# A gated mix of a state-space convolution and a squared-ReLU layer with all gradients: fifteen weight-gradient units moved ahead, inverse rows in load order, a denser pace of dense steps, later parameter gradients

## The chip, the cores and the metric

The kernel runs on one core of one Trainium2 chip. The metric is the device time of one execution in microseconds (us); lower is better. The engines are TensorE (PE; its weight loads PEld), VectorE (DVE), ScalarE (ACT), GpSimd (POOL) and SyncE (SP). DMAs are issued by SP, ACT or POOL, each in the order of its own program.

## The reference

The forward pass mixes two branches with a gate per position, and the reference returns its output and the gradients of fourteen inputs. x is 2048 x 448, the state-space part has 256 states per channel, the dense part 1792 hidden units, all in bf16.

```python
g = sigmoid((x * gate_w).sum(-1, keepdims=True))
# branch A: K[d, l] = Re(sum_n C[d, n] * exp(dt[d] * A[d, n] * l) * dt[d] * B[d, n])
#           y = irfft(rfft(x, 4096) * rfft(K, 4096))[:2048] + x * Dskip
# branch B: out = relu(x @ w1 + b1) ** 2 @ w2 + b2
out = g * a + (1 - g) * b
_out, _vjp = jax.vjp(_f, ...)      # then every gradient for grad_out
```

## The kernel before

**Layout.** Positions lie as 16 tiles of 128 (`LT`), channels as 448 columns (`D`); hidden units are 14 blocks of 128 (`FT`). Large SBUF tiles are reused by tag: a new tile of a tag waits until the last reader of the old one is done. The order of work of all engines from the first chunk on is written out by hand; nothing reorders it.

**The convolution.** It is a two-step transform over 64 x 64 positions. `fwd1` (L233) makes the first step in eight steps n = 0 to 7, each copied from PSUM by ACT and DVE (L207, L208, L217, L219) and stored to HBM (`gd`); `between(n)` (L1444) is called after each of them. `fwd2` (L254) loads it back and makes the second step. `cmul` (L266 to L271) multiplies spectra on DVE. `inv1` (L285) makes the first inverse step with the constant matrix `MI` and stores its rows to HBM (`hd`); `load_hs` (L294) loads a quarter of them with two DMAs, one for each half of the partitions, and `inv2` (L303) makes the second step. There are three inverses: `hd[0]` early, for the correlation that the filter's gradient needs (L660), `hd[1]` for the output `out_0`, and `hd[2]` for the gradient of x, `out_1`.

**The chunks.** The 14 chunks of 32 channels are worked in `period(c)`, L1158, c = 1 to 13, and a closing `period(14)`. In a chunk DVE builds two power tables X and Y by doubling (L707 to L721); TensorE turns them (L802, L816), multiplies them to kernel rows (`kgen`, L775), and forms the group products Z of the chunk before (L856), which DVE multiplies with a table (L872) and TensorE sums (L889) to the sums S and T. In the last chunk the kernel rows go to HBM (L790, `k_d`) and come back as the filter in `xs` (L1243); the transform of the filter, `fwd1` at L1448, follows `period(14)`. `s_out` (L906) stores S and T, and the parameter gradients load them later (`load_st`, L1359 and L1360).

**The dense steps.** `dense()` (L948) is a generator of 126 steps: the hidden units (L969), the projection (L996), the gradient of the hidden units (L1100) with its gate on DVE (L1076, `gate_rows`), and the projection back (L996 again). It keeps its results in HBM: hidden rows in `rT_d`, gated gradient rows in `dhT_d`, the branch rows of both projections in `br_d`. `De(x)` (L1127) raises the number of steps that are due by x and runs the steps that are missing. A live chunk asks for 9.7. `ahead()` (L1148), called in the last chunk behind the first half of the last table step, runs all that are left, loads the output gradient into `Gt`, a tile of tag U16 (L1153), and the first three blocks of hidden rows.

**The units.** Two weight gradients, `out_12` (from `rT_d`) and `out_10` (from `dhT_d`), are made in 125 units by the generator `units()`. `turn(i, th)` (L1268) transposes eight 128 x 128 pieces of block i to PSUM, and ACT or DVE copies them back (L1272, L1270); `mul_rows(i, th)` (L1281) makes eight matmuls of 448 columns; `turn_back` (L1298) turns a finished block of `out_10`. `Fl(n)` runs n units. All of them lie behind `period(14)`: ten in `between`, the rest between the steps of the tail, and `Fl(200)` at the end runs what is left. The first 14 blocks multiply with `DB2`, the output gradient scaled by 1 - g, which DVE makes from `Gt` in `between(0)` and `between(1)` (L1447) into a tile of tag Y16.

**The parameter gradients.** `param_grads(dt)` (L1371) is a generator of DVE work for four blocks of channels; its first instruction adds T to S (L1379). `Pg(n)` runs n of its segments: one after each of the eight steps of `fwd1`, and the rest before the products. Blocks 2 and 3 come with the last inverse; their tile `Dw`, of tag Y16, is loaded by SP (L1345) behind the product `GU` (L1573), which reads `Gt`, and ahead of the first `load_hs` of `hd[2]`.

**The tail in order.** `period(14)`, `fwd1` with `between`; loads; the products and `inv1` for `hd[1]`; the output loop with L1552 and L1553 and the branch rows (`load_br`, L1490); `GU` and the loads behind it; the loop for `out_1`; ten times a unit and a segment; two reductions (L1612); the rest of the units; the last small transposes (L1619, L1625) and stores.

## Time and profile before

| | us |
|---|---|
| median of 3 runs | 907.55 (905.39 to 908.53) |
| the profiled execution | 911.36 |
| its span, first to last instruction | 909.6 |

| stretch of the span | us | PE busy | DVE busy | ACT busy | granted clock | DMA share |
|---|---|---|---|---|---|---|
| start, spectra, first chunk: 0 to 217.4 | 217.4 | 131.7 | 160.4 | 134.5 | 0.72 | 0.79 |
| chunks 1 to 13: to 625.2 | 407.8 | 341.4 | 368.8 | 307.0 | 0.87 | 0.56 |
| closing period, filter to HBM and back: to 651.4 | 26.2 | 15.4 | 5.1 | 10.6 | 0.76 | 0.69 |
| transform of the filter: to 682.3 | 30.9 | 21.0 | 19.5 | 13.1 | 0.69 | 0.77 |
| products and first inverse: to 766.0 | 83.7 | 68.0 | 61.5 | 55.7 | 0.92 | 0.93 |
| output loop: to 822.0 | 56.0 | 47.0 | 37.2 | 24.9 | 1.00 | 0.93 |
| loop for the gradient of x: to 872.3 | 50.3 | 36.6 | 23.6 | 21.7 | 0.86 | 0.84 |
| end: to 909.6 | 37.3 | 25.7 | 13.6 | 11.8 | 0.91 | 0.15 |

How to read the profile: one execution on the chip, times in us from its start. L12 is line 12 of the kernel. "R<-hd" is a transfer or instruction that writes tile R and reads tensor hd. "[8.5 <-DMA P<-t_d]" behind an instruction is the idle time of its engine before it and what ended that. In rows of stretches the columns are the stretch, its length, busy time and number of instructions of PE, PEld, DVE, ACT and POOL, the granted TensorE clock as a share of full speed, the share of time in which the 16 DMA engines were busy, and GB/s. A row of a group gives the number of instructions, their busy time in us and the mean in ns, then the idle time before them. The chain of waits leads back from the last instruction to what released each step.

### The profile page before, as it was taken

Reading aid. Unit: us, or ns where it says so; the run is one execution under the profiler, and the core shown is the slowest. Engines: PE = TensorE matmul, PEld = TensorE weight load, DVE = VectorE, ACT = ScalarE, POOL = GpSimd, SP = SyncE. Lnnn points to the kernel's source line nnn. Section 1 sums busy time; section 2 is a strip of 40 time slices with the busy share of each in tenths; the row PEclk is TensorE's granted clock in tenths of the full one; section 3 lists DMA queues with packets and bytes.
Section 4 is the critical chain, followed back from the end, with each engine's and each line's share of the span. In section 5 each row is a group of like instructions: output and inputs, shape, how many; then the busy total and the mean of one; then the engine's idle time right before and its main releaser. Section 6 shows DMA issues by size and latency. Waiting matters only on the chain.

```text
span 909.6 us, 19275 instructions
## 1 busy us (share of the span) xinstructions
PE 686.9 (76%) x7785; PEld 356.3 (39%) x7785; DVE 689.6 (76%) x1184; ACT 579.4 (64%) x861; POOL 190.9 (21%) x301
## 2 busy tenths in 40 slices
PE   3757455676888789798879798886468887885985
PEld 2213111134354545454554455445234343433442
DVE  4786888775777998899999999984377947763670
ACT  0888567655777988897857666663436774353542
POOL 1233000320111312220312322122233311211211
PEclk9965655588787989999988987996669998998998
DMA  9798863895435845785455655663789999989831
GB/s 191 212 278 290 318 245 121 321 266 175 99 121 129 209 101 116 177 231 135 142 156 124 212 127 140 156 175 102 150 261 389 275 322 280 260 261 269 212 108 31
DMA packets 132920, 179.34 MB, mean 197 GB/s; under 512 B 67384, under 2 KB 106414, under 8 KB 132174
## 3 DMA queue, kind: packets, MB, share of 16 engines
q1 hardware_dynamic: 102458, 85.78, 36.6%
q0 software_dynamic: 22336, 71.95, 24.9%
q10 hardware_dynamic: 8036, 20.37, 6.3%
q8 instruction: 61, 1.00, 0.5%
q14 instruction: 29, 0.24, 0.1%
HBM read 95.13 MB, written 68.97 MB: 180 GB/s over the span
## 4 chain that ended last, share of the span: by engine, by line
PE 25%; issue 12%; DVE 9%; ACT 9%; DMA 8%; POOL 3%; SPq 1%; POOLq 0%; ACTq 0%; DVEq 0%
PE psX L1281 6%; PE psN L996 3%; PE psN L1100 3%; PE psF L816 2%; PE psX L775 2%; DVE Y L718 2%; DVE F L719 2%; DVE Y L721 1%; DMA k_d<-X 1%; DMA br_d<-D 1%; DMA rec<-rec_d 1%; ACT R L818 1%; DMA R<-sp 1%; ACT S L1109 1%; DMA R<-hd 1%
## 5 line engine op out<-in xcount | busy, mean ns | idle before, releaser
L996 PE MATMUL psN<-D,S 128*128 128x448 bf16 x448 | 101.0, 375 | 0.4 <-issue 0.4
L718 DVE TENSOR_TENSOR Y<-Y,F 128x256 bf16<-128x256 bf16 (+2 forms) x84 | 72.8, 866 | 4.7 <-ACT F L752 1.9
L721 DVE TENSOR_TENSOR Y<-Y,F 128x256 bf16<-128x256 bf16 (+2 forms) x84 | 72.8, 866 | 2.8
L719 DVE TENSOR_TENSOR F<-Y,F 128x256 bf16<-128x256 bf16 (+2 forms) x84 | 71.9, 856 | 1.0 <-ACT F L754 0.9
L861 ACT CAST R<-psF 128x1024 bf16<-128x1024 f32 x56 | 57.3, 1024 | 16.9 <-PE psF L856 15.4
L872 DVE TENSOR_TENSOR P<-R 128x2048 bf16<-128x2048 bf16 x42 | 49.4, 1219 | 20.3 <-ACT R L861 20.3
L996 PEld LDWEIGHTS <-S 128*128 128x128 bf16 x448 | 42.5, 103 | 45.8 <-issue 16.9
L1281 PEld LDWEIGHTS <-S 128*128 128x128 bf16 x448 | 42.7, 100 | 41.8 <-issue 11.7
L775 PE MATMUL psX<-X,Y 128*64 128x16 bf16 x1792 | 41.8, 188 | 19.6 <-DVE Y L721 18.9
L816 PE MATMUL psF<-ident,Y 128*128 128x128 bf16 x448 | 39.3, 258 | 19.3 <-ACT R L818 14.2
L1001 POOL DMA_DIRECT2D br_d<-D x32 | 17.8, 557 | 171.4 <-ACT D L1000 171.4
L1281 PE MATMUL psX<-Y,S 128*128 128x448 bf16 x224 | 50.0, 368 | 1.2 <-ACT S L1284 1.2
L818 ACT COPY R<-psF 128x2048 bf16<-128x2048 bf16 x15 | 28.0, 1869 | 34.8 <-PE psF L816 34.8
L1100 PE MATMUL psN<-S,U 128*128 128x512 bf16 x168 | 45.7, 407 | 5.2 <-ACT S L1109 4.9
L775 PEld LDWEIGHTS <-Y 128*64 128x64 bf16 x1792 | 40.0, 130 | 24.4 <-DVE Y L721 20.7
L1281 PE MATMUL psX<-D,S 128*128 128x449 bf16 x224 | 48.0, 358 | 2.1 <-ACT S L1287 1.9
L816 PEld LDWEIGHTS <-Y 128*128 128x128 bf16 x448 | 34.4, 118 | 24.2 <-issue 17.9
L707 DVE TENSOR_TENSOR X<-X,F 128x512 bf16<-128x512 bf16 (+1 forms) x70 | 37.5, 536 | 7.4 <-ACT F L746 4.7
L1272 ACT ACTIVATE S<-psN 128x1024 bf16<-128x1024 bf16 x28 | 28.8, 1028 | 22.4 <-PE psN L1268 22.4
L708 DVE TENSOR_TENSOR F<-X,F 128x512 bf16<-128x512 bf16 (+1 forms) x70 | 37.0, 528 | 2.4 <-ACT F L747 2.3
L969 PE MATMUL psN<-S,U 128*128 128x512 bf16 x120 | 34.5, 422 | 5.3 <-ACT S L962 2.9
L1109 ACT ACTIVATE S<-psN 128x512 bf16<-128x512 f32 x56 | 30.5, 600 | 10.7 <-PE psN L1103 10.7
(342 smaller groups left out, 1724.3 us busy)
## 6 DMA issues: line engine op xcount, KB each, us to landing
sp<-K ACTq DMA_DIRECT2D x8, 896.0 KB
S<-rT_d POOLq DMA_DIRECT2D x16, 448.0 KB, 7.6
dhT_d<-S POOLq DMA_DIRECT2D x28, 256.0 KB, 3.3
S<-rT_d POOLq DMA_DIRECT2D x14, 512.0 KB, 6.1
R<-sp SPq DMA_DIRECT2D x8, 896.0 KB
S<-dhT_d POOLq DMA_DIRECT2D x14, 512.0 KB, 5.9
R<-hd SPq DMA_DIRECT2D x16, 448.0 KB
rec<-rec_d SPq DMA_DIRECT2D x14, 480.0 KB
```

What stands on the lines that cost most here:

```text
L707: V.tensor_tensor(out=hi4, in0=lo, in1=bcast_dims(pr, [0, (None, n), 1]), op=ALU.mult)
L718: V.tensor_tensor(out=hi, in0=lo, in1=bcast_dims(pr, [0, (None, n // 2), 1]), op=ALU.mult)
L719: V.tensor_tensor(out=Vv.rearrange("p (x a q) -> p x a q", x=rows, q=2), in0=lo, in1=bcast_dims(pi, [0, (None, n // 2), 1]), op=ALU.mult)
L721: return V.tensor_tensor(out=T4[:, :, :, n:2 * n], in0=T4[:, :, :, n:2 * n], in1=V4, op=ALU.add)
L775: T_.matmul(ps[64 * jt:64 * jt + 64, ch * NA:ch * NA + NA], lhsT=Y[:, w, t, :], rhs=XW[:, 1 - t, w, :, 1], start=(k == 0), stop=(k == 3), ...
L816: T_.transpose(pt[:, h, i], Y[:, 16 * g + 8 * h + i].rearrange("p t b -> p (t b)"), ident[:])
L861: S.copy(zb[:, :, :, g % 2].rearrange("p s t n -> p t s n"), psz[:].rearrange("p t (s n) -> p t s n", s=2))
L872: V.tensor_tensor(out=pr.rearrange("p s t g n -> p s t (g n)"), in0=zv, in1=(xb if r == 0 else rev_dim(xb, 2)), op=ALU.mult)
L996: T_.matmul(ps[:, 0:D], lhsT=hb[j][:, P * tt:P * tt + P], rhs=ws[:, j, :], start=(w == 1 and j == 0), stop=(j == FT - 1))
L1100: T_.matmul(pss[k][:], lhsT=w2Tw[:, jp, dt, k], rhs=dblk[:, dt], start=(dt == 0), stop=False, skip_group_check=True)
L1109: S.mul(hblk[:, 2 * jp + k], pss[k][:], 2.0)
L1281: T_.matmul(ps[:, 0:w], lhsT=hn[i % 2][:, t, :], rhs=(DB2[:, t, :] if i < FT else U[:, t, 0:w]), start=(t == 0), stop=(t == LT - 1))
```

## The change

Five parts, all in one edit.

1. **Rows of the inverse.** The columns of `MI` are permuted, so that the rows of a quarter lie next to each other in `hd`; `load_hs` reads 8 x 448 contiguous elements per partition where it read four runs of 2 x 448. The branch rows lie in `br_d` by weight, partition and quarter, and `load_br` is one DMA of 4 x 448 elements per partition where it was two DMAs with two runs of 448 each.
2. **Pace.** `De` multiplies what it adds by 1.05.
3. **Units ahead.** The definitions of the units move ahead of the chunks. One unit runs after each of the first two table turns of the last chunk, one after the third, one after the fourth, one before its last sums; `period(14)` runs two after each of its four Z and one before each of its two sums: 15 in all. Until the chunks end (`early`) they use other PSUM banks; the turned pieces lie in four smaller buffers. `DB2` is loaded straight from the output gradient into U16 (eight DMAs on SP), when the last part of the projection back begins (`rows_ahead`), and DVE scales it in place behind the last table step (`scale_g`).
4. **A second load.** `Gt` is loaded again in the product loop (q = 2), into Y16, by eight DMAs on SP ahead of the first branch rows.
5. **Parameter gradients.** `between` runs no segment after the steps 0 to 3 and two after each of the steps 4 to 7.

The line `Fl(4 * FT + 2 - nf)` goes too; its argument was below zero there.

```diff
+    o_ = np.arange(64)
+    MI = MI[..., 16 * (o_ // 2 % 4) + 8 * (o_ // 32) + 2 * (o_ // 8 % 4) + o_ % 2]
     c["MI"] = MI.reshape(128, 2 * 128)
...
     def load_hs(self, hd, q, hs):
         for hp in range(2):
-            src = bass.AP(tensor=hd, offset=(8 * hp + 2 * q) * D, ap=[[64 * D, 64], [16 * D, 4], [1, 2 * D]])
+            src = bass.AP(tensor=hd, offset=(32 * hp + 8 * q) * D, ap=[[64 * D, 64], [1, 8 * D]])
...
-                                G_.dma_start(bass.AP(tensor=br_d, offset=(t * P * 2 + w) * D, ap=[[2 * D, P], [1, D]]), br)
+                                G_.dma_start(bass.AP(tensor=br_d, offset=(w * P * LT + 4 * (t // 2 % 4) + 2 * (t // 8) + t % 2) * D, ap=[[LT * D, P], [1, D]]), br)
...
-                if n_ == 1 and lb < 3:
-                    load_db(lb + 1)
+                if n_ == 1:
+                    load_db(lb + 1) if lb < 3 else rows_ahead()
...
+    FZ = 2
+    due, made, rate = 0.0, 0, 1.05
     def De(x):
-        due += x
+        due += x * rate
...
-    hr = [SB[:, 2048 * i:2048 * i + 2048] for i in range(3)]
-    hn = [SB[:, 6144 + 2048 * i:8192 + 2048 * i].rearrange("p (t f) -> p t f", f=P) for i in range(2)]
+    hr = [SB[:, o_:o_ + 2048] for o_ in (7168, 0, 2048)]
+    hn = [[SB[:, o_:o_ + 1024].rearrange("p (t f) -> p t f", f=P) for o_ in oo] for oo in ((4096, 5120), (6144, 9216))]
...
+    def rows_ahead():
+        nonlocal DB2
+        DB2 = K.t("U16", [P, LT, D])
+        for g in range(NG):
+            for h in range(2):
+                nc.sync.dma_start(flat(DB2[32 * g:32 * g + 32, 8 * h:8 * h + 8]), thalf(G2, g, h))
+        rows_in(0)
+
+    def scale_g():
+        for t in range(LT):
+            V.tensor_scalar(out=DB2[:, t, :], in0=DB2[:, t, :], scalar1=omg32[:, t:t + 1], scalar2=None, op0=ALU.mult)
     def ahead():
         De(1000)
-        Gt = K.t("U16", [P, LT, D])
-        for g in range(NG):
-            nc.sync.dma_start(flat(Gt[32 * g:32 * g + 32]), tl(G2, g))
...
-        for i in range(3):
+        for i in range(1, 3):
             rows_in(i)
...
             for k in range(4):
                 Z(k)
+                Fl(FZ)
...
             De(1)
+            if last:
+                ahead()
             step_y(4, 0)
             for g in range(2):
                 YTs.setdefault(c, []).append(load_yt(g) if not last else turn_yt(g, None))
+                if last:
+                    Fl(1)
...
-            if last:
-                ahead()
             De(1)
             step_y(4, 1)
+            if last:
+                scale_g()
...
             YTs[c].append(turn_yt(2, None))
+            if last:
+                Fl(1)
...
             YTs[c].append(turn_yt(3, None))
+        if c >= NCH - 1:
+            Fl(1)
         p_sum(c - 1, Q, (0, 1))
         Q = p_mul(XTs[c - 1][1], zbs[1])
         De(1.1)
+        if c >= NCH - 1:
+            Fl(1)
         p_sum(c - 1, Q, (2, 3))
...
     def between(n):
-        if n < 2:
-            for t in range(8 * n, 8 * n + 8):
-                V.tensor_scalar(out=DB2[:, t, :], in0=Gt[:, t, :], scalar1=omg32[:, t:t + 1], scalar2=None, op0=ALU.mult)
         Fl(1 if n < 6 else 2)
-        Pg(1)
+        if n > 3:
+            Pg(2)
...
-        for h in range(2):
-            nc.sync.dma_start(t_[:, h], bass.AP(tensor=br_d, offset=((2 * q + 8 * h) * P * 2 + w) * D, ap=[[2 * D, P], [P * 2 * D, 2], [1, D]]))
+        nc.sync.dma_start(t_.rearrange("p h x d -> p (h x d)"), bass.AP(tensor=br_d, offset=(w * P * LT + 4 * q) * D, ap=[[LT * D, P], [1, 4 * D]]))
...
         if q == 2:
+            Gt = K.t("Y16", [P, LT, D])
+            for g in range(NG):
+                for h in range(2):
+                    nc.sync.dma_start(flat(Gt[32 * g:32 * g + 32, 8 * h:8 * h + 8]), thalf(G2, g, h))
             brq = [load_br(0, k) for k in range(3)]
...
     V.tensor_tensor(out=GU, in0=Gt[:], in1=Uv, op=ALU.mult)
-    Fl(4 * FT + 2 - nf)
     Dw = K.t("Y16", [P, 8192])
```

`thalf(ap, g, h)` is the half of `tl(ap, g)`: eight tiles of 32 partitions.

More of the change, by code (lines that the diff above doesn't have):

```diff
@@ new lines @@
+    for (p0, p1) in ((0, 16), (64, 128), (32, 64), (16, 32)):
+        offs = vp[p0] - LT * p0
+        assert all((vp[p] - LT * p == offs).all() for p in range(p0, p1))
+        runs, j = [], 0
+        while p0 > 0 and j < LT:
+            n_ = int((offs == offs[j]).sum())
+            runs.append((j, n_, int(offs[j])))
+            j += n_
+        ones = [r for r in runs if r[1] == 1][:4]
+        if len(ones) == 4:
+            assert all((b_[0] - a_[0], b_[2] - a_[2]) == (4, 4) for a_, b_ in zip(ones, ones[1:]))
+            reload(p0, p1, ones[0][0], ones[0][2], m=4)
+            runs = [r for r in runs if r not in ones]
+        for j, n_, of in runs:
+            reload(p0, p1, j, of, rep=n_)
+        if p0 == 0:
+            nc.sync.dma_start(flat(xs[0:p1]), bass.AP(tensor=k_d, offset=0, ap=[[LT * D, p1], [1, LT * D]]))
```

213 lines of the change are left out of this document (99 added, 114 removed).

## The prediction

> **What bounds the kernel now.** I read the busy time by stage first, with the granted TensorE clock (PEclk) and the share of the DMA engines in its last columns.
>
> ```profile
> 258.20:290.80 32.60, 29.89 (x417) 15.56 (x417) 27.16 (x39) 26.65 (x37) 5.50 (x11) 0.87 0.47 130
> 407.80:435.60 27.80, 24.26 (x422) 14.58 (x422) 26.98 (x40) 22.57 (x31) 1.80 (x3) 0.94 0.60 146
> 590.50:625.20 34.70, 27.21 (x306) 15.74 (x306) 30.11 (x44) 18.98 (x22) 6.11 (x9) 0.80 0.49 127
> 628.50:651.40 22.90, 12.07 (x353) 8.82 (x352) 5.03 (x6) 9.93 (x11) 8.84 (x16) 0.75 0.79 175
> 651.40:682.30 30.90, 21.03 (x110) 11.12 (x111) 19.47 (x47) 13.07 (x19) 7.72 (x13) 0.69 0.77 235
> 682.30:822.00 139.70, 114.98 (x845) 57.24 (x844) 98.61 (x172) 80.60 (x129) 34.21 (x63) 0.95 0.93 296
> 872.30:909.60 37.30, 25.72 (x178) 13.65 (x174) 13.58 (x35) 11.81 (x28) 6.87 (x12) 0.91 0.15 46
> ```
>
> The first three rows are chunks 2, 7 and 13. Chunk 7 is VectorE's: 26.98 of 27.80 us. Chunk 2 is 4.8 us longer with the same VectorE work, because TensorE is full (29.89 of 32.60). The last chunk is 34.70 us long and no engine fills it. The fourth and fifth rows, from the kernel row sums to the end of their transform, run at half-empty engines and a clock of 0.75 and 0.69. After them TensorE carries most of the time, and the last row is almost TensorE alone. The chain of waits then says what links the last chunk to the transform (start, us, what):
>
> ```profile
> 622.92 5.69 PE psN L996 x21
> 628.61 2.17 PE psX L775 x128
> 632.45 7.12 DMA k_d<-X
> 640.23 5.97 DMA F<-k_d
> 646.25 1.23 DVE M L872
> 648.56 2.91 issue
> 651.46 0.91 PE psN L233 x2
> ```
>
> Three dense steps (5.69 us) stand ahead of the row sums of the last chunk, L775. Those go to HBM and come back as the filter, and the transform, L233, begins 22.9 us after L775 did. TensorE has little to do meanwhile. The next link is VectorE's, here in order of time:
>
> ```profile
> 663.59 0.69 DVE L1379 TENSOR_TENSOR P<-P 128x512 f32<-128x512 f32 x1 [8.52 <-DMA P<-t_d]
> 664.20 0.62 DVE L208 CAST D<-psN 128x448 bf16<-128x448 f32 x1
> 664.74 1.08 DVE L219 CAST D<-psF 128x896 bf16<-128x896 f32 x1
> 665.74 2.15 DVE L1447 TENSOR_SCALAR Y<-U,omg 128x448 bf16<-128x448 bf16 x8
> ```
>
> The first instruction of the parameter gradients, L1379, waits 8.52 us for the sums T to land (P<-t_d). Queued behind it are the transform's PSUM copies (L208 and L219, 1.70 us for a step), so TensorE stops too.
>
> **The change part by part.** The sum is made against the profiled execution: 911.36 us, 909.6 of them span. The median of the runs is 907.55, so 3.8 comes off at the end.
>
> *A, rows in the order of their loads.* The two half loads of each inverse quarter become one contiguous run per partition in place of four; the branch rows become one DMA in place of two.
>
> ```profile
> 213.84 1.16 DVE L219 CAST st<-psN 128x448 bf16<-128x448 f32 x2 [4.50 <-PE psN L660]
> ```
> ```profile
> L303 PE MATMUL psN<-R,cb_Etw 64*32 64x448 bf16 x64 | 6.3, 386 | 12.4 <-DMA R<-hd 12.4
> ```
>
> Early, VectorE waits 4.50 us for L660, which consumes the first four of these loads, and everything later hangs on it: gain 0 to 4.5, taken 4, since four runs per partition become one in a busy stretch. The later loads cost TensorE 12.4 us of waiting; that is booked in F.
>
> *B, pace 1.05.* A live chunk asks for 9.7 dense steps, now 10.185, so 0.485 more. Three steps took 5.69 us above, one at most 1.9, so a chunk gets 0.9 us of TensorE work more. Where VectorE bounds the chunk this costs nothing; its cover is TensorE's 3.5 idle us (chunk 7), and without that it costs the 0.9. In full chunks such as chunk 2 it costs 0.9. With about half of the twelve chunks like that, the bounds are 0 and 5; taken 2.5. What it buys is C: all 126 steps are out before the middle of the last chunk, not after it.
>
> *C, the way to the row sums.* The 5.69 us go. Two weight-gradient units (transposes) stand there instead: the first lies in the wait for the scalar engine's copy between two table turns, the second costs at most 1.06 (below). That is 4.6. The last chunk also leaves VectorE 4.6 us idle (34.70 less 30.11), against 0.8 in chunk 7. These waits come with the gate steps that now fall a chunk earlier, where their own time is paid as before. So up to 8.4; taken 7. The scaling of the output gradient, 16 instructions or two times 2.15 us, moves to VectorE right behind the last table step. Queued behind it are the products:
>
> ```profile
> 624.01 1.22 DVE L872 TENSOR_TENSOR M<-R 128x2048 bf16<-128x2048 bf16 x1
> ```
> ```profile
> 635.51 0.40 PE L889 MATMUL psS<-P,cb_sel 128*32 128x256 bf16 x1
> ```
>
> The last ended at 625.23 and L889 read the first at 635.51, so 10 us hide the scaling; it costs 4.3 if that cover goes. The extra rows of loads (eight DMAs on SP for the gradient, POOL's first unit rows) are issued when the tile comes free in the chunk before, ahead of nothing urgent.
>
> *D, units between the row sums and the transform.* Fifteen units move out of the tail. Two are in C; thirteen, seven transposes and six products, now stand on TensorE between L775 and L233. Their prices, cold and warm:
>
> ```profile
> 666.57 1.06 PE L1268 MATMUL psS<-ident,S 128*128 128x128 bf16 x8
> ...
> 670.07 3.19 PE L1281 MATMUL psX<-Y,S 128*128 128x448 bf16 x8
> ...
> 682.79 0.61 PE L1268 MATMUL psS<-ident,S 128*128 128x128 bf16 x8
> 683.58 1.67 PE L1281 MATMUL psX<-Y,S 128*128 128x448 bf16 x8 [0.17 <-ACT S L1284]
> ```
>
> Warm they are 7 x 0.61 + 6 x 1.67 = 14.3 us, cold 7 x 1.06 + 6 x 3.19 = 26.6. TensorE is busy 12.07 of the 22.9 us today. So the stretch becomes 26.4 warm to 38.7 cold if the units fill the gaps, 3.5 to 15.8 more than the 22.9. I take 8, nearer the warm end: fed without gaps, the clock stands at 0.95 (sixth row). The filter's round trip is then covered. Row loads for the units sit on POOL's queue behind the filter's reloads; the only unit that needs such a late one is the fifteenth.
>
> The Trainium skill, "TensorE: Matmul & The Clock Gate", section "Part 1: The HAM clock gate", says that about 3.4 us of sustained work release the clock and an idle window of that length halves it again. The trace agrees: 0.75 and 0.69 where TensorE is half idle, 0.95 where it is fed. By the rule D would be some 5 us, not 8; but it speaks against B, as early dense steps leave the second half of the last chunk idle, so that the row sums could run cold.
>
> *E, later parameter gradients.* L1379 moves from behind the first of the transform's eight steps to behind the fifth. Today T is there 15.0 us after the sums end (663.59 less 648.56). Five warm steps take about 13.5 (eight matmuls of the width of L1281's, 1.67, and a unit, 1.1 in the mean, for each), so 1 to 2 us of the 8.52 remain. The work behind that is mostly triples of
>
> ```profile
> L1385 DVE TENSOR_TENSOR X<-X,P 128x256 f32<-128x256 f32 x20 | 7.6, 419 | 0.2
> ```
>
> Ahead of the last step's copies stand six segments, two light ones (0.7) and four of three instructions (1.26), and with the copies of three steps (1.70) that is 11.5 us. From the sums' end, where the transform would now start, to the last copy that makes 26.5; from the transform's start it was 30.9. At best the whole wait and the scaling, 8.5 + 4.3, go; at worst nothing. Taken 4.
>
> *F, transfers in the tail.* The gradient is loaded a second time, into Y16, and so the parameter tile that follows there must wait for its last reader, L1573. SP issues in order, and the loads of the last inverse are behind it.
>
> ```profile
> 820.98 0.46 SPq L1345 DMA_DIRECT2D Y<-in_A_A_re_dram  x1
> ```
> ```profile
> 822.95 3.89 DVE L1573 TENSOR_TENSOR K<-U,D 128x7168 bf16<-128x7168 bf16 x1
> ```
> ```profile
> 833.21 2.64 SPq L294 DMA_DIRECT2D R<-hd  x4
> ```
> ```profile
> 839.65 0.56 PE L303 MATMUL psN<-R,cb_Etw 64*32 64x448 bf16 x4 [8.54 <-DMA R<-hd]
> ```
>
> SP starts 5.9 us later (826.84 less 820.98). Its sixteen loads took 12.2 us; sixteen at the 0.46 of the row would be 7.4. So 1 to 6 us arrive at TensorE's 8.54 us wait. Against that stand faster loads there and in the other waits of the 12.4. The second load itself is
>
> ```profile
> U<-in_grad_out_dram SPq DMA_DIRECT2D x4, 448.0 KB
> ```
>
> 1.8 MB, 6 us at the 296 GB/s of the sixth row, issued a stage before it is read. Between -4 and +12; taken +1.
>
> *G, the end.* Every stage of the tail asks for as many units as before, so the fifteen are missing at the end.
>
> ```profile
> 872.25 1.69 PE L1281 MATMUL psX<-D,S 128*128 128x449 bf16 x8
> ...
> 883.31 3.19 PE L1612 MATMUL psN<-K,g_b 128*1 128x448 bf16 x16
> ...
> 899.36 0.22 PE L1619 MATMUL psN<-ident,dlog_b 128*4 128x128 bf16 x1
> ```
> ```profile
> 887.71 0.07 DVE L1391 DVE_READ_ACCUMULATOR X<-X,dtc 64x1 f32 x1
> ```
>
> From the last inverse output to L1619 it is 27.1 us. Left are three units and the last turn back, two of them products at 1.69 and two far shorter, say 4.9, and two reductions of 3.19: 11.3, which is 15.8 less. But L1619 also needs VectorE's last gradient, at 887.78 today, which makes 888.5 and 10.9 less if VectorE comes no sooner. It waits there for unit transposes that will be over, so it should come sooner. Taken 14.
>
> Sum: -4 +2.5 -7 +8 -4 +1 -14 = -17.5. 911.36 becomes 893.9; from the median, 890.
>
> **The rivals.** *Cold units.* The clock stays low through the last chunk's end and the transform: the units pay 26.6 us and, each waiting for a copy in turn, fill no gap, so the transform starts 49.5 us after L775 and E gains nothing. Then -4 +2.5 -7 +26.6 +1 -14 = +5, 912.5. For it: clock 0.75 and 0.69 there. Against: those are the clocks of a starved engine. It decides from a start about 45 us after L775.
>
> *The tail keeps its time.* VectorE's gradients and SP's order set the end: G is 10.9, F +6, E 0. Then -4 +2.5 -7 +8 +6 -10.9 = -5.4, 902. For it: 887.71 lies far from 872.25. Against: VectorE waits for TensorE there.
>
> *It does not do what it says.* The pace and units only exchange work of one engine: total TensorE work is the same, and the transfer part is hidden, so within 0.3%, 907. Against: idle TensorE in the fourth row.
>
> *Better.* Warm units (+3.5), E -8, F -4, G -15.8: -4 +2.5 -7 +3.5 -8 -4 -15.8 = -32.8, 875.
>
> **How the numbers follow.** About 0.3%, 2.7 us, is what a measurement of this kernel can tell from no change; its runs spread over 0.35%. Chances: forecast 0.62, tail keeps its time 0.16, better 0.07, no effect 0.05, cold units 0.10. Hence faster 0.85, same 0.05, slower 0.10. The terms' half widths, about 2, 2.5, 2, 6, 6, 8 and 2.5, combine to 12.5: 878 to 902 for the likeliest. The range 872 to 908 takes in the better case, the kept tail and no effect.
>
> **What would show it.** Right: L996 gone before L775; TensorE above 0.8 busy between L775 and L233 with clock near 0.9, L233 25 to 32 us after L775; L1379 waiting under 4 us; L660 done before 210; L1619 about 11 us after the last inverse output; the first parameter load right behind L1573. Wrong: L233 over 40 us after L775; a period of chunks 2 to 12 above today's by more than a microsecond each; a longer wait at L303; or VectorE alone at the end.

## The result, and the profile after

The changed kernel takes 903.78 us (median of 20 runs, 896.16 to 916.40), the kernel before 908.88 (20 runs, 901.60 to 913.24). The ratio is 0.9934 with a 95% interval of 0.9908 to 0.9960: about 6 us faster, where 17.5 were forecast. The direction was right; the size was a third of the forecast.

The first profiled execution of the changed kernel was a disturbed one (span 913.4). In its chunk 5 VectorE waited for a transposing load of rows, in the view of who waited for whom, in us, times, longest:

```profile
DVE Y L762 <- DMA R<-Y: 13.5, 1, 13.5
```

A second profile of the same kernel (run e1_again, span 900.2) has no such wait there, and is read below. Lines have moved: L775 is now L780 (row sums), L996 L1001, L233 L235 (transform), L207/L208 L209/L210, L238 L240 (its stores), L266 L268 (products), L285 L287, L289 L291, L294 L296 (row loads), L301 L303 and L303 L305 (second inverse step), L660 L665, L1268 L1155 (unit transposes), L1270 L1157, L1281 L1168, L1345 L1372, L1379 L1406, L1573 L1601 (`GU`), L1076 L1081 (the gate) and L1109 L1114 (the copy that it reads), L1612 L1639, L1619 L1646.

Stretches of the second profile, in the columns of before, and two rows of the kernel before that were not shown:

```profile
408.00:599.00 191.00, 154.75 (x2474) 91.18 (x2490) 178.51 (x264) 133.99 (x187) 45.58 (x69) 0.93 0.56 152
599.00:625.30 26.30, 21.11 (x289) 14.10 (x286) 25.47 (x49) 16.31 (x18) 3.24 (x6) 0.82 0.66 152
625.30:649.50 24.20, 22.11 (x457) 15.04 (x457) 10.62 (x15) 18.93 (x21) 10.57 (x18) 0.99 0.82 183
649.50:708.90 59.40, 42.76 (x280) 22.58 (x280) 38.90 (x90) 29.37 (x43) 18.51 (x34) 0.86 0.89 305
708.90:769.50 60.60, 44.05 (x303) 20.53 (x300) 40.03 (x42) 35.30 (x59) 8.45 (x15) 0.89 0.92 280
769.50:828.90 59.40, 50.50 (x368) 24.49 (x368) 38.17 (x80) 26.18 (x55) 13.92 (x25) 0.94 0.86 259
828.90:848.90 20.00, 7.71 (x64) 4.49 (x62) 4.44 (x2) 4.92 (x11) 2.44 (x4) 0.80 0.82 232
848.90:877.70 28.80, 26.68 (x195) 11.80 (x196) 17.98 (x45) 16.71 (x39) 4.54 (x8) 0.90 0.73 181
877.70:900.20 22.50, 12.20 (x66) 5.51 (x66) 12.44 (x34) 5.10 (x13) 5.51 (x10) 0.90 0.21 55
```
```profile
407.80:590.50 182.70, 155.46 (x2448) 90.84 (x2448) 175.68 (x259) 129.88 (x179) 40.67 (x61) 0.88 0.56 151
711.70:766.10 54.40, 43.24 (x299) 20.60 (x296) 38.28 (x39) 36.71 (x56) 8.94 (x16) 0.91 0.91 280
```

| stretch | before | changed | difference | forecast |
|---|---|---|---|---|
| to the first seed of chunk 1 | 217.4 | 217.8 | +0.4 | A -4 |
| chunks 1 to 6 | 190.4 | 190.2 | -0.2 | B |
| chunks 7 to 12 | 182.7 | 191.0 | +8.3 | B +2.5 in all |
| last seed to row sums | 38.0 | 26.3 | -11.7 | C -7 |
| row sums to transform | 23.0 | 24.2 | +1.2 | D +8 |
| transform to first product | 60.2 | 59.4 | -0.8 | E -4 |
| first product to first row of `out_0` | 54.4 | 60.6 | +6.2 | F |
| to `GU` | 56.9 | 59.4 | +2.5 | none |
| `GU` to first row of the last inverse | 16.6 | 20.0 | +3.4 | F |
| to the last inverse output | 32.7 | 28.8 | -3.9 | F +1 in all |
| end | 37.3 | 22.5 | -14.8 | G -14 |
| span | 909.6 | 900.2 | -9.4 | -17.5 |

(The profile of before lies 2.5 us above its median of 20, so the span shows 9.4 where the medians of these runs show 7.) The waits of the prediction stand as follows in the second profile: two rows of VectorE, one of ScalarE, one of TensorE. Behind them is one row of the kernel before that was not shown, VectorE's wait for R<-sp.

```profile
667.41 0.69 DVE L1406 TENSOR_TENSOR P<-P 128x512 f32<-128x512 f32 x1 [8.74 <-DMA P<-t_d]
...
754.49 1.09 DVE L268 TENSOR_TENSOR X<-R,K 128x1792 bf16<-128x1792 bf16 x1 [18.51 <-DMA R<-sp]
```
```profile
672.52 0.53 ACT L209 CAST D<-psN 128x448 bf16<-128x448 f32 x1 [10.01 <-DMA gd<-D]
```
```profile
848.85 0.56 PE L305 MATMUL psN<-R,cb_Etw 64*32 64x448 bf16 x4 [12.11 <-DMA R<-hd]
```
```profile
751.97 1.09 DVE L266 TENSOR_TENSOR X<-R,K 128x1792 bf16<-128x1792 bf16 x1 [13.85 <-DMA R<-sp]
```

The wait for T is as long as it was (8.52 us before), only four steps of the transform later. ScalarE waits 10 us for the store that frees a stage buffer of the transform. The wait for R<-sp in the product loop has grown from 13.9 to 18.5, TensorE's at the last inverse from 8.54 to 12.11. The other three are waits for transfers that are new or have grown. One more wait has grown and is not for a transfer: VectorE's in chunks 7 to 12, in the view of who waited for whom (before, then changed):

```profile
DVE S L1076 <- ACT S L1109: 2.2, 2, 1.5
```
```profile
DVE S L1081 <- ACT S L1114: 8.2, 7, 2.3
```

The gate on VectorE waits there for ScalarE's copy of the gradient of the hidden units.

### The profile page after: what moved, and what is told of

It reads as the page before. It is cut to its first block, busy times and chain, and to the rows that moved or that the text cites. A ratio compares the mean times of both kernels' runs of the same rounds, so it can differ in the third digit from the quotient of the medians.

```text
span 913.4 us, 19283 instructions
## 1 busy us (share of the span) xinstructions
PE 684.2 (75%) x7785; PEld 355.6 (39%) x7785; DVE 689.7 (76%) x1184; ACT 579.2 (63%) x861; POOL 190.8 (21%) x301
## 5 line engine op out<-in xcount | busy, mean ns | idle before, releaser
L1001 PE MATMUL psN<-D,S 128*128 128x448 bf16 x448 | 102.1, 378 | 1.1 <-ACT S L1056 1.1
L1168 PEld LDWEIGHTS <-S 128*128 128x128 bf16 x448 | 43.4, 102 | 45.4 <-issue 16.1
L780 PE MATMUL psX<-X,Y 128*64 128x16 bf16 x1792 | 42.4, 188 | 24.9 <-DVE Y L726 24.2
L1001 PEld LDWEIGHTS <-S 128*128 128x128 bf16 x448 | 43.1, 104 | 46.2 <-issue 16.3
L1168 PE MATMUL psX<-D,S 128*128 128x449 bf16 x224 | 51.5, 377 | 1.9 <-ACT S L1175 1.9
L780 PEld LDWEIGHTS <-Y 128*64 128x64 bf16 x1792 | 40.3, 130 | 30.2 <-DVE Y L726 26.7
L821 PE MATMUL psF<-ident,Y 128*128 128x128 bf16 x448 | 39.7, 259 | 13.5 <-ACT R L823 10.3
L1159 ACT ACTIVATE S<-psN 128x1024 bf16<-128x1024 bf16 x33 | 33.8, 1024 | 19.0 <-PE psN L1155 19.0
L1168 PE MATMUL psX<-U,S 128*128 128x448 bf16 x176 | 39.4, 369 | 1.1 <-ACT S L1172 1.1
L1114 ACT ACTIVATE S<-psN 128x512 bf16<-128x512 f32 x56 | 30.5, 597 | 12.9 <-PE psN L1108 12.9
```

Source lines behind the costliest of these rows:

```text
L780: T_.matmul(ps[64 * jt:64 * jt + 64, ch * NA:ch * NA + NA], lhsT=Y[:, w, t, :], rhs=XW[:, 1 - t, w, :, 1], start=(k == 0), stop=(k == 3), ...
L821: T_.transpose(pt[:, h, i], Y[:, 16 * g + 8 * h + i].rearrange("p t b -> p (t b)"), ident[:])
L1001: T_.matmul(ps[:, 0:D], lhsT=hb[j][:, P * tt:P * tt + P], rhs=ws[:, j, :], start=(w == 1 and j == 0), stop=(j == FT - 1))
L1168: T_.matmul(ps[:, 0:w], lhsT=hn[i % 2][th][:, t - 8 * th, :], rhs=(DB2[:, t, :] if i < FT else U[:, t, 0:w]), start=(t == 0), stop=(t == L ...
```

## Experiments

Times are medians in us; the changed kernel has 903.78, or 902.18 in its repeat. Each ratio is to the kernel before, timed on the same chip. An interval here is about 0.35% to each side, so 3 us between two versions are not told apart by one pair of times. Their stretches are read from one profile each, or from the mean of the profiles of several versions, where the text says so. "Theory 1" and "rival" are those of the text quoted ahead of each result, which was written before the run.

**The changed kernel again (e1_again).** No edit.

> The changed kernel once more, unaltered, for a second profile. In the profiled execution of it chunk 5 was 41.3 us long (31.1 before), with one wait of 13.5 us of VectorE's L762 for the transposing load R<-Y. Theory 1, a disturbance of that execution: chunk 5 is 28 to 32 us here, the span about 900, and the other stages repeat: chunks 1 to 12 without chunk 5 some 12 us longer than before, last seed to row sums 26 us (38.1 before), VectorE's longest wait for R<-sp about 19 us (13.9 before), first L305 of the last inverse about 19 us after GU's end (12.8 before). Theory 2, the denser pace makes the load late: the wait stands here again, in that chunk or another, and the span is over 908. Ratio to before 0.990 to 0.997.

902.18, ratio 0.9923 (0.9893 to 0.9953). Chunk 5 took 27.9 us and the other stretches repeated, so the long wait was a disturbance of that execution: theory 1.

**The row order alone (e8_row_order_alone).** The kernel before with the new `MI`, `load_hs`, `br_d` and `load_br`.

> The kernel before with the row order alone: the permuted columns of MI, contiguous row loads and branch rows. Theory 1: early nothing, since L660 never waits for these loads but stands behind dense steps (first seed of chunk 1 at 217 +-1.5), and in the tail at most 1 to 3 us (TensorE's waits for R<-hd 12.4 in total before): 0 to 3 us faster than before. Rival, the forecast's term A and its gain of F: chunk 1 starts 4 us sooner and the tail gains up to 4: 5 to 8 us faster than before.

908.94, ratio 0.9997 (0.9972 to 1.0022), and the first seed of chunk 1 stands at 216.5 us. That is theory 1. The view of tile hd of the kernel before says why (us, times, who waited for it):

```profile
who waited for it (us, times):
  PE psN L303: 12.4, 4
  DVE st L208: 1.5, 1
  ACT st L207: 1.3, 1
```

L660 is not in it: it stands among hidden units and the first chunk's work in TensorE's program, and never waited for a row. The waits of L303 in the tail (12.4 us in all) are 10.6 us with the new order, and the time did not shrink.

**The pace (e4_old_pace, c5_last_version_denser_pace).** The old pace on the changed kernel, and the reverse, the denser pace on c2 (below):

```diff
-    due, made, rate = 0.0, 0, 1.05
+    due, made, rate = 0.0, 0, 1.0
```

> The changed kernel with the old pace (a factor of 1.0 in place of 1.05): nine dense steps are left at the start of the last chunk and run ahead of the last table step. Theory 1, pace and shorter last chunk exchange the same work: chunks 1 to 12 get 8 to 12 us shorter, last seed to row sums 8 to 15 us longer, and the time is that of the changed kernel within 3 us. Rival, the forecast's terms B and C (+2.5 and -7): 4 to 8 us slower than the changed kernel. Second rival, the pace costs more than it brings: 3 to 6 us faster.

896.76, ratio 0.9882 (0.9844 to 0.9920).

> The fastest version (no second load, rows of the last inverse ahead, parameter loads earlier, raw loads on ScalarE) with the pace of 1.05 again in place of 1.0. Theory 1, the pace shifts dense steps from the last chunk into chunks 7 to 12 and costs there what it brings: first seed of chunk 1 to that of chunk 13 some 10 us longer (371.1 with the old pace, about 382 here), last seed to row sums some 7 us shorter (33.1, about 26 here), and 880 to 886 for the whole, 0 to 5 slower. Rival, forecast (+2.5 for the chunks, 7 back behind them): 3 to 6 us faster, 875 to 878.

885.65, ratio 0.9745 (0.9708 to 0.9783), against 880.86 and 882.78 with the old pace. The rows of e4_old_pace for chunks 7 to 12 and from the last seed to the row sums:

```profile
405.30:589.70 184.40, 156.72 (x2460) 93.27 (x2474) 175.58 (x257) 131.10 (x181) 40.49 (x61) 0.87 0.56 150
589.70:621.60 31.90, 26.27 (x326) 15.50 (x325) 29.92 (x58) 19.12 (x24) 8.81 (x14) 0.96 0.66 183
```

Over the profiles of all runs, the time from the first seed of chunk 1 to that of chunk 13 is 382.7 in the mean of nine at 1.05 (the disturbed one left out), and 373.7 in the mean of eight at 1.0: the pace costs 9.0. From there to the row sums it is 26 with it; with the old pace it is 38.1 in the kernel before and 33.1 in the mean of six versions that have the rest of the change. So of the 12 us that the last chunk lost, the pace made 7 and the rest of the change 5 (argued, not shown: the earlier place of `ahead`, which no run undid alone), and the pace costs about 2 more than it brings. Both pairs of times point the same way (3 to 7 us), each hardly beyond its intervals.

The profiles also show what the pace costs in chunks 7 to 12. In all nine profiles with it VectorE runs 55 gate instructions there and waits 8.2 to 12.2 us in front of them (10.3 in the mean); in all eight with the old pace it runs 45 and waits 2.1 to 4.4 (2.9). For e4_old_pace:

```profile
DVE S L1081 <- ACT S L1114: 3.8, 2, 3.2
```

The ten more gates are 3 us of work (178.51 us of VectorE against 175.58), and in the mean 7 us more are waiting in VectorE's order. Why the denser pace puts more gates right behind their copies was not examined.

**The way of T (e5_gradients_behind_transform, e12_gradients_as_before, e11_raw_loads_on_act).** No segments inside the transform; one after each step, as before; and the changed kernel with six loads on another queue:

```diff
-        nc.sync.dma_start(pr2[:, :, i], src[0:2 * P].rearrange("(t p) n -> p t n", p=P))
+        nc.scalar.dma_start(pr2[:, :, i], src[0:2 * P].rearrange("(t p) n -> p t n", p=P))
```

> The changed kernel with no segment of the parameter gradients inside the transform of the filter; all of them follow it. In the second profile of the changed kernel L1406 waits 8.7 us for the sums T behind the fifth step, and TensorE's sixth step 7.6 us behind that. Theory 1, T's way through HBM sets this point, not the place of L1406: the transform takes 17 to 19 us in place of 25.7, but VectorE's gradients still begin when T lands (667.4 there) and need 29 us and some copies, so the first product comes at most 3 to 5 us sooner and the kernel is 2 to 5 us faster than the changed one. Rival, the 8 us of TensorE come through: the first product 8 us sooner, 6 to 8 us faster. Second rival: the gradients are all that counts, the first product within 1 us, no change.

910.29, ratio 1.0019 (0.9991 to 1.0047), 6 to 8 us more than the changed kernel: all three theories fell. The transform stayed at 26.4 us, since its seventh step waits for a store:

```profile
672.44 0.53 ACT L209 CAST D<-psN 128x448 bf16<-128x448 f32 x1 [11.10 <-DMA gd<-D]
```

and the first product came 40.4 us behind it (33.7 in the changed kernel): VectorE's gradients began later, at 675.8 us in place of 667.4, and TensorE stood still for a store in place of T.

> The changed kernel with one segment of the parameter gradients after each of the transform's eight steps, as in the kernel before. Theory 1: the transform stalls at its second step for T instead of the sixth, as before (L1406 waits 15 to 17 us less the time that has passed), but both places end on the same landing of T and VectorE's 29 us behind it: transform start to first product 58 to 61 us (58 in the changed kernel, 60.2 before), the time within 3 us of the changed kernel. Rival, the forecast's term E: 4 us or more slower in that stretch.

902.66, ratio 0.9934 (0.9896 to 0.9971). Theory 1: from transform start to first product it is 60.8 us, against 57.2 to 59.4 in eight profiles that have the later gradients and the old queue for the six loads. That is 1 to 4 us, where the forecast had 4, and in the time it does not show.

> The changed kernel with the six loads of A, B and C for the parameter gradients (L1390) issued by ScalarE in place of SP. In the changed kernel SP issues the last stores of S and T, these six loads, four loads of S and T and a constant from 650.0 to 661.7 (second profile), and only then the transform's stores gd<-D; ScalarE's seventh step waits 10.0 us for one of these (a stage buffer). Theory 1, SP's order sets this point as much as T does: the first gd<-D is issued 2 to 4 us sooner, T lands 2 to 4 us sooner, the transform falls from 25.7 to 21 to 24, the kernel is 2 to 4 us faster than the changed one. Rival, T's way through HBM alone: L1406 still starts 18 us after the row of S and T stores begins, the transform stays within 1 us, no change.

900.49, ratio 0.9914 (0.9880 to 0.9948). The transform took 22.2 us, as theory 1 said. The queue of SP around it, in the second profile of the changed kernel and in this run:

```profile
654.55 0.53 SPq L1390 DMA_DIRECT2D X<-in_A_A_re_dram  x1
...
659.20 0.43 SPq L1387 DMA_DIRECT2D P<-t_d  x1
...
663.65 3.47 SPq L240 DMA_DIRECT2D gd<-D  x4
```
```profile
654.53 1.15 SPq L911 DMA_DIRECT2D t_d<-st  x2
...
656.35 0.43 SPq L1387 DMA_DIRECT2D P<-t_d  x1
...
658.38 4.62 SPq L240 DMA_DIRECT2D gd<-D  x4
```

The transform starts at 649.5 in the one and at 651.0 in the other. Its first stores, whose steps are long done, are issued 7.4 us behind that in place of 14.1; L1406 starts 11.8 us behind it in place of 17.9 and no longer waits for T; and the wait for a stage buffer falls to 4.2 us. So SP's order held the transform as well as T. In the whole that is within the interval.

**The second load (e2_second_load_earlier, e10_no_second_load).** The eight DMAs of `Gt` ahead of the product loop; and none at all, with

```diff
-    V.tensor_tensor(out=gp[:], in0=g_b[:], in1=omg_b[:], op=ALU.mult)
+    V.reciprocal(ds32g[:], omg32[:])
+    V.tensor_tensor(out=gp[:], in0=g32[:], in1=ds32g[:], op=ALU.mult)
...
-                V.scalar_tensor_tensor(out=jk, in0=ps, scalar=1.0, in1=Gt[:, t, :], op0=ALU.mult, op1=ALU.mult, accum_out=dg[:, t:t + 1])
+                V.scalar_tensor_tensor(out=jk, in0=ps, scalar=1.0, in1=DB2[:, t, :], op0=ALU.mult, op1=ALU.mult, accum_out=dg[:, t:t + 1])
...
-    V.tensor_tensor(out=GU, in0=Gt[:], in1=Uv, op=ALU.mult)
+    V.tensor_tensor(out=GU, in0=DB2[:], in1=Uv, op=ALU.mult)
```

> The second load of the output gradient (eight DMAs on SP) is issued ahead of the product loop, where SP has nothing to issue for 25 us, in place of at q = 2. Theory 1, SP's order: in the changed kernel these eight DMAs keep SP for 9.8 us (734.15 to 743.95), and the stores of hd and the next R<-sp stand behind them; moved away, R<-sp is issued 6 to 8 us sooner, VectorE's wait falls from 19.3 to 12 to 14 us, and the kernel is 5 to 8 us faster than the changed one (ratio to before 0.985 to 0.989). Rival, bandwidth: 1.8 MB more cost 6 us of a stretch in which the DMA engines are full, wherever they are issued: then fwd2 and the first product come 4 to 6 us later instead and the time is that of the changed kernel within 2 us.

903.58, ratio 0.9914 (0.9876 to 0.9952). VectorE's wait for R<-sp fell to 10.8 us, but one of 7.4 for TensorE stood ahead of it, and the product stretch (first product to first row of `out_0`) stayed at 62.4 us. SP's order at this place was not the cause. The rival is right in the time, not in the place: the first product did not come later. The early load found no free time. From 685 to 735 us the share of the DMA engines is 1.02 in this run, and the eight issues, 9.9 us in the changed kernel, took 22.

> The changed kernel without the second load of the output gradient: L1580 and GU take the scaled rows DB2, which stay in U16, and the factor 1 - g is divided out in the weights of 128 x 16 that follow (g / (1 - g) for GU, g for the gate). The tag Y16 is then free, and the loads of the parameter gradients no longer wait for GU. Theory 1, bandwidth: those 1.8 MB and the eight issues cost the stretch from the first product to the first L305 6 to 8 us (60.7 in the second profile of the changed kernel, 54.4 before): it falls to 53 to 56, and GU to the last inverse's first L305 from 16.1 to 11 to 13; 7 to 11 us faster than the changed kernel. Rival, other transfers that the change has brought into this stretch (unit rows, in another order) make it long: it stays above 58, and 3 to 5 us come from the parameter loads alone.

889.20, ratio 0.9763 (0.9733 to 0.9792), 13 to 15 us less than the changed kernel. The product stretch, the loop of `out_0` and the stretch behind `GU`:

```profile
703.60:757.30 53.70, 41.62 (x301) 20.32 (x300) 40.30 (x43) 35.20 (x59) 8.46 (x15) 0.94 0.89 284
757.30:813.30 56.00, 46.91 (x366) 23.26 (x366) 38.19 (x79) 26.14 (x54) 13.84 (x25) 1.00 0.87 264
813.30:832.60 19.30, 8.01 (x62) 4.61 (x60) 4.52 (x3) 4.92 (x11) 2.46 (x5) 0.79 1.02 285
```

The product stretch is 6.9 us shorter: theory 1 at this place. Over all profiles it is 61.4 us in the mean of seven with the load (the disturbed one left out) and 54.8 in the mean of five without it (c8 below left out), at an equal number of units ahead. With DMA engines 0.9 busy, 1.8 MB are 6 us at 300 GB/s, and they show. The stretch behind `GU` is only 0.7 us shorter, where theory 1 had 3 to 5: the sixteen parameter loads no longer wait for `GU`, but they still stand ahead of the rows. Another 3 us come from the clock in the loop of `out_0` (below), and 5.9 ahead of chunk 1, where this edit changes nothing and no cause was found; so the edit explains 7.6 us of this profile at its two places, and 13 is the difference of the medians.

**The rows of the last inverse first (e3_last_rows_first).** `hsn = load_hs(2, 0)` moves from behind the sixteen parameter loads to ahead of them.

> The two DMAs of the first quarter for the last inverse are issued ahead of the sixteen loads of the parameter gradients, and so do not wait behind GU's reading. Theory 1, TensorE's wait there sets the end: first L305 of the last inverse comes 15 us or more sooner (about 845 in place of 862.8 in the profiled execution's time, 5 after GU's end in place of 19), and the kernel is 4 to 10 us faster than the changed one. Rival, VectorE's parameter gradients set the end: their loads still wait for GU and now stand behind two more DMAs, the last VectorE gradient (902.1 there, against 904.07 for the end of the reductions) moves by -1 to +2 and the time stays within 2 us of the changed kernel, though TensorE starts sooner.

894.22, ratio 0.9829 (0.9792 to 0.9865), 8 us less than the repeat of the changed kernel on the same chip: theory 1. `GU` to the first row is 8.1 us in place of 20.0; 7.6 of these 11.9 are lost again in the loop (36.4 against 28.8), where the next rows now wait behind the parameter loads. So 4.3 us of the 7.9 between the two spans stand at the edit's place; the others lie ahead of `GU`, where nothing was changed.

```profile
825.30:833.40 8.10, 7.92 (x65) 4.59 (x63) 4.49 (x2) 4.66 (x11) 2.44 (x5) 1.00 1.02 330
833.40:869.80 36.40, 27.18 (x196) 11.98 (x196) 18.84 (x48) 17.14 (x40) 4.54 (x8) 0.86 0.74 211
```

VectorE's last gradient ends at 881.7, 11.9 behind the last inverse output; L1646 follows at 883.6.

**The parts together (c1, c2, c7).** c1 is no second load, rows first, old pace; c2 has also the six loads on ScalarE, and the parameter loads of the last two blocks, but for S and T of block 3, issued in the third quarter of the output loop. c7 is c2 again.

> Three parts together: no second load of the output gradient, the rows of the last inverse ahead of the parameter loads, the old pace of 1.0. Alone they made 13, 8 and 5 to 7 us on the changed kernel. Theory 1, they sit at three places and add except that the second and the first share GU's wait: 20 to 25 us faster than the changed kernel, 877 to 884. Rival, VectorE's gradients then end last (881.7 against 869.8 for the inverse in the run with the rows first): 14 to 18 faster, 885 to 889.

884.57, ratio 0.9737 (0.9696 to 0.9778): the rival's lower end. The gains of the medians do not add. At their own places the parts had made 7.6, 4.3 and about 2 us, and the same stretches are 12 us shorter in c1 than in the second profile of the changed kernel, so there they nearly do.

> As the run before, and further: the six loads of A, B and C on ScalarE, and the loads of the parameter gradients of blocks 2 and 3 (all but S and T of block 3) issued after the third quarter of the output loop, since Y16 is free there. Theory 1, VectorE's last gradients wait for their loads: they start 4 to 8 us sooner, L1646 stands 8 to 12 us behind the last inverse output, and it is 3 to 8 us faster than the run before (872 to 880). Rival, the DMA engines are full there (0.9 busy), so the inverse's rows and unit rows come later by as much: within 2 us of the run before.

880.86, ratio 0.9693 (0.9649 to 0.9736). L1646 still stands 13.8 us behind the last inverse output, so theory 1 fell there, and the 3.7 us that were gained are within the interval.

**The units (e7_units_back, c6_last_version_units_back, c8_copies_on_scalar).** Eight of the fifteen go back to the end (`FZ = 0`), on the changed kernel and on c2:

> The changed kernel without the two units behind each of the four Z of the closing period: eight units go back to the end of the tail, seven stay ahead. Theory 1, those units stand in the wait for the filter and are nearly free there: row sums to transform goes from 24.2 to 21 to 23, last inverse output to the last transposes from 13.8 to 22 to 24, and the kernel is 6 to 9 us slower than the changed one. Rival, the forecast's term D (13 units cost 8): row sums to transform falls to 18 to 20 and the loss is 3 to 5.

903.65, ratio 0.9907 (0.9871 to 0.9944): no difference from the changed kernel, so theory 1 fell, and the rival's loss of 3 to 5 did not show. The end is 7.9 us longer (30.4), but row sums to transform is 1.5 us shorter (22.7) and the product stretch 3.4 shorter than the mean of 61.4 (58.0).

> The fastest version without the two units behind each Z of the closing period: eight units go back to the end. On the changed kernel the same edit cost 7.8 us at the end and the time did not move, since the stretch from the first product to GU was 2 to 6 us shorter. Theory 1, those eight units are worth 5 to 8 us, and what hid it there was the crowd of transfers around the second load, which is gone here: row sums to transform 1.5 us shorter, the end 7 to 8 us longer, the stages between within 1.5 us, 884 to 889 for the whole against 881. Rival, the units that stand in the product and output loops (those of out_10 in place of out_12) cost there what is saved at the end: these stages 3 to 6 us shorter, the whole within 3 us of 881.

> The fastest version once more, unaltered, as the measure for the run before: 878 to 884. Its two loops (first product to first L305, and from there to GU) repeat within 1 us (53.7 and 58.2) if they differ from the units' kernel by the units; by 2 to 3 us more or less if the granted clock moves them.

c6 has 882.17, ratio 0.9705 (0.9649 to 0.9760); c7 has 882.78, ratio 0.9712 (0.9659 to 0.9764). That is the rival. In c6 the end is 30.5 us in place of 22.6, but row sums to transform is 22.4 (24.6 in c2, 26.2 in c7), the product stretch 51.1 (53.7, 54.4), the loop of `out_0` 56.0 (58.2, 59.2). The loop proves little, since it moves by as much between profiles of one kernel (last section). The product stretch does more. It is 61.4 with the load and the eight units, 58.0 without the units, 54.8 without the load and 51.1 without both: the load costs 6.6 to 6.9 us there, the units 3.4 to 3.7, and the two add (61.4 and 54.8 are the means above, the others one profile each). TensorE and VectorE in the product stretch of c7 show what the units do:

```profile
745.78 0.61 PE L1155 MATMUL psN<-ident,S 128*128 128x128 bf16 x8
746.22 1.68 PE L1168 MATMUL psX<-D,S 128*128 128x449 bf16 x8
753.24 1.01 PE L1155 MATMUL psS<-ident,S 128*128 128x128 bf16 x8 [5.33 <-DVE S L1157]
754.04 3.21 PE L1168 MATMUL psX<-D,S 128*128 128x449 bf16 x8
```
```profile
745.97 1.09 DVE L268 TENSOR_TENSOR X<-R,K 128x1792 bf16<-128x1792 bf16 x1 [10.74 <-DMA R<-sp]
...
752.50 0.68 DVE L1157 COPY S<-psS 128x1024 bf16<-128x1024 bf16 x1
```

With the units ahead, the first blocks of `out_10` are reached here, and VectorE copies half of their transposes. The copy stands behind a product that waits for R<-sp; TensorE waits 5.33 us for the copy, and its next two units cost 4.2 us in place of 2.3. (This is what the Trainium skill, "TensorE: Matmul & The Clock Gate", section "Part 1: The HAM clock gate", says of an idle window: the clock is halved until about 3.4 us of work have passed.) c8 is c2 with

```diff
-        if i >= FT and th == 0:
+        if i >= FT + 4 and th == 0:
             V.tensor_copy(hn[i % 2][th][:], ps[:])
```

> The fastest version with ScalarE in place of VectorE copying the turned halves of the first four blocks of out_10 (L1157, for i below 18). In its repeat TensorE waited 5.3 us for such a copy, which stands behind two products of VectorE that wait 10.7 us for R<-sp, and ran the next unit cold (1.01 and 3.21 us in place of 0.61 and 1.68). Theory 1, this is what the units ahead give back in the product loop: the wait is gone, product to first L305 falls from 53.7 and 54.4 to 50 to 52 (51.0 with the units back), the whole 2 to 4 us faster, 877 to 880. Rival, the products wait for R<-sp all the same and set that stretch: within 1 us in it, no change in the whole.

878.92, ratio 0.9658 (0.9627 to 0.9689). The product stretch is 50.2 us and TensorE's longest single wait in it 1.6: the wait and its cause are shown. Little of it reached the whole in this profile, where the loop of `out_0` took 61.1 us (58.2 in c2, 59.2 in c7) at a clock of 0.91. The time is 2 to 4 us under c2 and c7, within the interval. It is the fastest version: 3.4% under the kernel before.

## Why only a third of the forecast came

Against the forecast, in us of the two profiles, B came out 5.6 worse, F 4.7, A 4.4, E 3.2, and the loop of `out_0`, which had no term, 2.5; D came out 6.8 better, C 4.7 and G 0.8. That makes the 8.1 between -17.5 and -9.4. It was luck that the miss was not larger: without the better D and C it would have been 19.6, more than was forecast.

- **F failed**, and to undo it brought the most. The second load was taken as nearly free ("issued a stage before it is read", taken +1 with all else in F), though its 6 us had been worked out. At a DMA share of 0.93, in the forecast's own row, the engines had no time for it: the load costs 6.6 to 6.9 us in the product stretch, and an earlier issue did not hide it (e2). The rows of the last inverse came 3.4 us later, within the 1 to 6 that were named, and the loop behind them was 3.9 shorter, so F as a whole was 5.7. There was no gain from faster rows (e8).
- **A failed** at "L660, which consumes the first four of these loads": L660 reads them but never waited for them. It made +0.4 in place of -4.
- **B failed** in its mechanism: 8 to 9 us in place of 2.5, beyond its bound of 5, and not where it was expected. It was to cost 0.9 us in each chunk that TensorE fills, such as chunk 2, and nothing where VectorE bounds the chunk. Chunks 1 to 6 kept their time (-0.2). Chunks 7 to 12, which VectorE bounds (175.68 of 182.7 us before), took 8.3 us more: the dense steps bring gates there that run on VectorE, 2.8 us of more work and 6 us of more waiting for ScalarE's copies. The cover that was named, TensorE's idle 3.5 us, is the wrong engine's.
- **C was mis-sized** the other way, -11.7 in place of -7: the pace took the gates out of the last chunk and made 7 of it (VectorE's work fell from 30.1 to 25.5 us), and the rest of the change made 5. C's gain from the pace is bought with B: B and C together were -3.6, where -4.5 was forecast.
- **D was mis-sized**, +1.2 in place of +8, and below its warm bound of 3.5. The thirteen units took what was forecast, but TensorE's own 12.07 us in that stretch had been measured at a clock of 0.75; fed, at 0.99, they and the units together were 22.11. By the rule of the Trainium skill, "TensorE: Matmul & The Clock Gate", section "Part 1: The HAM clock gate", D was some 5, as the prediction worked it out; the measurement is under that too. The warning about cold row sums that the prediction drew from the same page also came true, for little: TensorE was busy for 8.03 of the 13.2 us ahead of them, and they took 2.48 us at a clock of 0.85, where before they took 2.22 at 1.00.
- **E** was -0.8 to -3 in place of -4. The step that failed is "1 to 2 us of the 8.52 remain". Five warm steps took 9 us (649.5 to 658.7), not 13.5, since a step of the transform has four matmuls (0.9 us), where the forecast counted eight; T was there 18 us after the sums' end, not 15; and the wait was 8.74. Behind it stood a second one that the forecast did not see: SP issues the stores of the transform behind eighteen other DMAs (e11).
- **G was right at its place** (-14.8 for -14), but "every stage of the tail asks for as many units as before" counted units and not which ones: the stages between met other blocks, with copies on VectorE. For eight of the units the times with and without them ahead are the same (e7, c6): the 7.9 us at the end are given back, 3.4 to 3.7 of them in the product stretch, 1.5 to 4 between row sums and transform; the rest is not told apart from the noise of the loops.

The rival "the tail keeps its time" came out at 902, next to the result, and in part by luck. Its F (+6) was nearly right and E was small; its G was not, since TensorE's last units and reductions, not VectorE, ran last (VectorE's last gradient ends at 890.6, L1646 starts at 891.5), and it had the wrong A, B, C and D of the forecast. Of what was to show the forecast right, TensorE was 0.91 busy between row sums and transform, and the first parameter load stood right behind `GU`. A wait of L1379 under 4 us did not come, L1646 stood 13.8 us behind the last inverse output and not 11, and a longer wait at L303, listed as wrong, did come.

## What to carry to other kernels

Where the DMA engines are 0.9 busy, do not count on an early issue to hide more bytes: here they cost their time in both places that were tried. First look for an algebraic way not to load them (here a factor per position, divided out of 16 columns). Work moved along a fixed order shifts all work behind it: ask which units now meet which engine's queue, not how many are left at the end. Before a denser pace is called free, look at every engine that the added step uses, and at what it waits for there. And a load that is read late may not be late itself: look who waits for it.

## What was not expected of the hardware

The output loop of the changed kernel took 56.0 us at a granted clock of 1.00 in its first profile and 59.4 at 0.94 in its second, with 46.91 and 50.50 us of TensorE. Its rows in the second profile tell where the clock fell:

```profile
800.10:803.50 3.40, 2.36 (x20) 0.67 (x17) 2.56 (x7) 3.40 (x7) 0.05 (x1) 0.99 1.00 382
803.50:806.90 3.40, 3.40 (x14) 1.23 (x14) 2.13 (x6) 0.20 (x1) 0.00 (x0) 0.50 1.00 315
820.50:823.90 3.40, 2.07 (x24) 1.04 (x22) 2.00 (x5) 0.63 (x2) 0.00 (x0) 1.00 0.32 109
823.90:827.30 3.40, 3.40 (x16) 1.67 (x14) 0.82 (x3) 1.37 (x2) 2.73 (x5) 0.51 0.49 142
```

It was half for 3.4 us, twice, each time right behind a stretch of the same length in which TensorE was busy for only 2.36 or 2.07 us. In e10_no_second_load a stretch with 2.07 (807.3 to 810.7 us) was not followed by this, so an idle third of such a stretch goes with the fall but does not settle it; what does was not found. Two such falls are the 3 us by which these profiles differ in the loop.

In one profiled execution VectorE waited 13.5 us for a transposing load; in the other seventeen its longest such wait is 3.1 us. Nothing in its rows names a cause.
